# Layer 1's second half in quarters, its first product for two token blocks from seven block products

## The chip, the cores and the metric

The kernel runs on one core of one Trainium2 chip. The metric is the device time of one execution in microseconds (us): 603.91 us, the median of three runs (602.19 to 604.12).

## The reference

```python
attn_out = _attn_ref(**attn_kwargs)          # 2 batches, 8 heads, 768 tokens, head size 64; window of 16 and block maxima
x = attn_out.transpose(0, 2, 1, 3).reshape(B * S, H * D)      # 1536 tokens x 512
...
h = x @ w_in                                 # layer 1: 512 -> 2048
g = h * np.clip(h + 3.0, 0.0, 6.0) / 6.0
x = g @ w_out                                # 2048 -> 512
...
h = x @ w_in                                 # layer 2, other weights
g = h * (1.0 / (1.0 + np.exp(-h)))
return (g @ w_out).astype(np.float32)
```

The weights of both layers arrive as 64-bit floats.

## The kernel before

**Precision.** Every operand of a wide matmul is kept as two 32-bit parts, a high part (a rounded copy) and a low part (value minus high part). A product of two operands is three matmuls, high x high, high x low and low x high, summed in one bank. So `hidden` (line 720), the first product of one slice of 128 hidden units for one block of 512 tokens, is 4 pieces of the inner size 512 times 3 = 12 matmuls of 128x512, issued as two halves of 6. `project` (lines 790 to 817), the second product of that slice, is 4 output groups x 3 = 12 matmuls.

**Stages.** Attention fills the first part; its results are turned into layer 1's input `x` (lines 699 to 717). Then come the two layers. A layer's 2048 hidden units are 16 slices, in two halves of 8. `STEPS` lists (layer, half, first token, tokens, slice) for all 96 pieces of work. Layer 1's first half runs block by block over its 8 slices, and so does its second half, over the token blocks 2, 0, 1. Layer 2 runs its halves in quarters of 4 slices: a quarter goes through blocks 2, 0, 1 before the next quarter starts. One `chunk` is the stretch of pieces that is summed in the same four accumulator banks; when it ends, the banks are emptied into `acc` in the local memory: `finish` with half 0 copies (ScalarE), `finish` with half 1 adds (VectorE, line 869, with a sixth as factor in layer 1) and for layer 1 also writes the high part of layer 2's input, `finish_lo` (line 880) the low part; `fold` (line 854) adds layer 2's early quarters.

**Seven block products.** In layer 2, blocks 0 and 1 don't go through `hidden`. Two slices of hidden units, split by the two halves of the inner size, are a 2x2 arrangement of weight blocks; the two token blocks, split the same way, are a 2x2 arrangement of inputs. Their product is formed from seven products instead of eight (`FACTORS`, `prod` on line 947), each 2 pieces x 3 = 6 matmuls. Their operands are partly sums: four weight sums per pair of slices (`ssum`, line 915, VectorE, 128x256; high parts `s_hi` on line 934, low parts `s_lo` on line 941) and four token sums per layer (`tsum` on line 897, `t_hi`, `t_lo`, 128x1024). Seven joins on VectorE (`join`, line 971: `u2`, `vee`, `u4`, `c22`, `c21`, `c12`, `c11`) and one copy (`keep`) turn seven products into the four results `k`, `v`, `u`, `d` of a pair. From there `act` (ScalarE, sigmoid or relu), `gate` (VectorE), `gate_hi` (mostly ScalarE) and `gate_lo` (VectorE, line 786) make the two parts of the operand of `project`. Layer 1 applies `act` and `gate` to a bank directly (line 769), the block products' results lie in the local memory (line 764).

**Weights.** `fetch` loads 64-bit words (SP), five steps on ScalarE and VectorE turn them into 32-bit values in `bits`, `conv_hi` copies the high part into a weight buffer and `conv_lo` subtracts (GpSimd on line 467, or VectorE).

**What sets the order.** Nothing is reordered: every engine executes its instructions in the order in which `PROGRAM` lists the operations. `ORDER` is that list, written out in the source; a star sends a copy to VectorE that ScalarE would do, or a `conv_lo` or `normal` to VectorE instead of GpSimd. Eight banks are shared by all products, taken and freed in that order (`Ring`), and so are the buffers of gates (`gs`), values (`rs`) and weights (`ws`). `grow` turns memory that has become free into more of these buffers.

```python
STEPS += [(0, 1, j * WIDE, WIDE, f) for j in BLOCKS for f in range(HALF)]
STEPS += [
    (1, half, j * WIDE, WIDE, q * QUARTER + f)
    for half in range(2)
    for q in range(2)
    for j in BLOCKS
    for f in range(QUARTER)
]
FACTORS = {
    1: ("w", 0, 0, "x", 0, 0),
    2: ("w", 0, 2, "x", 0, 2),
    3: ("s", 3, 0, "x", 1, 2),
...
```

Of the kernel before, what the change touches and what calls it, by code (L numbers as in the profile page):

```python
# [168 lines left out]
hidden 8 1, act 8, conv_sign 16, conv_clamp 16, conv_join 16, finish 0 0 0 2, mix 17, gate 8, hidden 9 1,
hidden 11 1, conv_hi 16, inverse 19, normal 19*, turn 19, mixed_hi 17*, gate_hi 8*, gate_lo 8, load_v 16, mix  # L170
16, keys 21, mixed_hi 16, mixed_lo 16, scores 21, masked 21, turned 19, keys 23*, turn 18, fetch 17, conv_low
17, act 9, gate 9, exps 21, guard 21, hidden 10 0, hidden 10 1, inverse 21, normal 21*, gate_hi 9, gate_lo 9,
grow 1, turned 18, conv_sign 17, load_v 19, mix 19, conv_mag 17, conv_clamp 17, conv_join 17, conv_hi 17*,
# [974 lines left out]
```

## Time and profile before

| | us |
|---|---|
| median of three runs | 603.91 |
| the profiled execution | 602.95 |
| its span (first to last instruction) | 601.1 |
| TensorE busy (3164 matmuls) | 590.1 |
| VectorE busy | 476.4 |
| ScalarE busy | 261.3 |
| GpSimd busy | 86.1 |

The profile names engines PE (TensorE), DVE (VectorE), ACT (ScalarE), POOL (GpSimd) and SP (transfers); PEld is TensorE's loading of weights. Busy is the time in which at least one instruction of the engine ran; a matmul's recorded duration overlaps the next one's, so the pace of a stream is read from starts. The granted TensorE clock is 1.00 in every slice of 20 us from 20 us on.

### The profile page before, as it was taken

Reading aid. Unit: us, or ns where it says so; the run is one execution under the profiler, and the core shown is the slowest. Engines: PE = TensorE matmul, PEld = TensorE weight load, DVE = VectorE, ACT = ScalarE, POOL = GpSimd, SP = SyncE. Lnnn points to the kernel's source line nnn. Section 1 sums busy time; section 2 is a strip of 40 time slices with the busy share of each in tenths; the row PEclk is TensorE's granted clock in tenths of the full one; section 3 lists DMA queues with packets and bytes.
Section 4 is the critical chain, followed back from the end, with each engine's and each line's share of the span. In section 5 each row is a group of like instructions: output and inputs, shape, how many; then the busy total and the mean of one; then the engine's idle time right before and its main releaser. Section 6 shows DMA issues by size and latency. Waiting matters only on the chain.

```text
span 601.1 us, 8713 instructions
## 1 busy us (share of the span) xinstructions
PE 590.1 (98%) x3164; PEld 489.4 (81%) x3164; DVE 476.4 (79%) x1047; ACT 261.3 (43%) x614; POOL 86.1 (14%) x97
## 2 busy tenths in 40 slices
PE   7899999999999999999999999999999999999997
PEld 7778788888888888888888888888888788888886
DVE  4999999587697867955446799998989888988865
ACT  4898778664322324421223435344434233421330
POOL 3583330200001012000000100010100310121000
PEclk9999999999999999999999999999999999999999
DMA  9999965231323223202000202123123122120023
GB/s 249 262 216 259 213 168 111 71 99 26 95 70 106 81 95 106 71 5 66 1 0 1 70 1 70 36 70 106 39 67 105 37 70 71 31 75 1 1 87 123
DMA packets 69051, 51.56 MB, mean 86 GB/s; under 512 B 36368, under 2 KB 63504, under 8 KB 69008
## 3 DMA queue, kind: packets, MB, share of 16 engines
q1 hardware_dynamic: 69008, 51.01, 31.5%
q8 instruction: 25, 0.41, 0.3%
q14 instruction: 18, 0.15, 0.1%
HBM read 47.85 MB, written 3.15 MB: 85 GB/s over the span
## 4 chain that ended last, share of the span: by engine, by line
PE 86%; DVE 7%; ACT 4%; DMA 1%; issue 1%; SPq 0%; DVEq 0%; ACTq 0%
PE bank L730 27%; PE bank L806 22%; PE bank L809 19%; PE bank L966 11%; PE bank L622 2%; PE bank L691 2%; PE bank L679 1%; PE bank L517 1%; DMA early_w<-in_k_dram 1%; DVE g L786 1%; PE bank L1063 1%; ACT early_units L651 1%; ACT early_w L651 1%; DVE kmax L531 1%; DVE early_w L637 1%
## 5 line engine op out<-in xcount | busy, mean ns | idle before, releaser
L730 PE MATMUL bank<-x,w 128*128 128x512 f32 x576 | 139.8, 392 | 0.0
L806 PE MATMUL bank<-g,w 128*128 128x512 f32 x576 | 137.9, 392 | 0.0
L809 PE MATMUL bank<-w,g 128*128 128x512 f32 (+1 forms) x588 | 136.3, 385 | 0.4 <-DVE g L786 0.3
L809 PEld LDWEIGHTS bank<-w,g 128*128 128x128 f32 x588 | 108.7, 188 | 23.3 <-DVE g L786 1.3
L806 PEld LDWEIGHTS bank<-g,w 128*128 128x128 f32 x576 | 107.1, 188 | 22.2
L730 PEld LDWEIGHTS bank<-x,w 128*128 128x128 f32 x576 | 107.2, 188 | 22.0 <-DVE x L714 0.2
L467 POOL TENSOR_TENSOR w<-bits,w 128x512 fp32r<-128x512 f32 x26 | 36.1, 1391 | 324.0 <-ACT w L463 161.4
L786 DVE TENSOR_TENSOR g<-r,g 128x512 fp32r<-128x512 f32 x72 | 52.9, 739 | 16.9 <-ACT g L780 15.5
L759 ACT ACTIVATE r<-bank 128x512 f32<-128x512 f32 x60 | 35.4, 596 | 67.2 <-PE bank L730 50.6
L423 ACT ACTIVATE mag<-words 128x512 f32<-128x512 f32 x64 | 42.9, 671 | 43.8 <-DVE bits L445 16.9
L769 DVE SCALAR_TENSOR_TENSOR r<-r,bank 128x512 f32<-128x512 f32 x48 | 32.7, 683 | 21.2 <-ACT r L759 21.0
L780 ACT CAST g<-r 128x512 fp32r<-128x512 f32 x43 | 26.7, 621 | 52.1 <-PE bank L806 16.1
L730 PE MATMUL bank<-x_late,w 128*128 128x512 f32 x192 | 44.7, 389 | 0.0
L730 PEld LDWEIGHTS bank<-x_late,w 128*128 128x128 f32 x192 | 36.0, 188 | 7.5
L966 PE MATMUL bank<-w,x 128*128 128x512 f32 x144 | 35.7, 389 | 0.0
L452 DVE SCALAR_TENSOR_TENSOR bits<-words,bits 128x512 uint32<-128x512 uint32 x48 | 34.8, 725 | 0.7
L439 DVE TENSOR_SCALAR mag<-mag 128x512 f32<-128x512 f32 x64 | 28.5, 445 | 7.9 <-ACT mag L423 7.5
L445 DVE SCALAR_TENSOR_TENSOR bits<-mag,bits 128x512 uint32<-128x512 uint32 x48 | 33.1, 689 | 1.0
L966 PEld LDWEIGHTS bank<-w,x 128*128 128x128 f32 x144 | 27.0, 188 | 5.6
L651 ACT ACTIVATE early_w<-early_w,stat 128x120 f32<-128x120 f32 x72 | 27.5, 385 | 4.0 <-DVE stat L637 3.9
L467 POOL TENSOR_TENSOR w<-cst,w 128x512 fp32r<-128x512 f32 x10 | 14.3, 1425 | 88.2 <-ACT w L463 44.0
L432 DVE TENSOR_SCALAR bits<-words 128x512 uint32<-128x512 uint32 x48 | 22.0, 460 | 3.5 <-DMA words<-in_moe_w_in_dram 1.8
(144 smaller groups left out, 768.3 us busy)
## 6 DMA issues: line engine op xcount, KB each, us to landing
words<-in_moe_w_in_dram SPq DMA_DIRECT2D x32, 512.0 KB, 3.9
words<-in_moe_w_out_dram SPq DMA_DIRECT2D x32, 512.0 KB, 3.4
early_r<-in_v_dram SPq DMA_DIRECT2D x15, 192.0 KB, 4.5
out_dram<-acc SPq DMA_DIRECT2D x11, 256.0 KB, 2.0
early_w<-in_q_dram SPq DMA_DIRECT2D x10, 256.0 KB, 6.0
stage<-in_k_dram SPq DMA_DIRECT2D x3, 512.0 KB, 5.2
stage<-in_v_dram SPq DMA_DIRECT2D x3, 512.0 KB, 7.2
early_w<-in_v_dram SPq DMA_DIRECT2D x3, 512.0 KB, 5.5
```

Source lines behind the costliest of these rows:

```text
L423: nc.scalar.activation(out=out, in_=low_high(h)[:, 1].bitcast(F32), func=AF.Abs, scale=EXP_SHIFT)
L445: nc.vector.scalar_tensor_tensor(out=bits, in0=mags.use(h).bitcast(U32), scalar=3, in1=bits, op0=ALU.logical_shift_left, op1=ALU.bitwise_or,)
L452: nc.vector.scalar_tensor_tensor(out=bits, in0=low_high(h)[:, 1], scalar=0x80000000, in1=bits, op0=ALU.bitwise_and, op1=ALU.bitwise_or,)
L467: eng.tensor_tensor(out=w_half(h, 1), in0=bitss.use(h).bitcast(F32), in1=w_half(h, 0).bitcast(F32), op=ALU.subtract,)
L651: nc.scalar.activation(out=pr[:, hp], in_=pr[:, hp], func=AF.Exp, scale=-1.0, bias=st[:, 0, hp : hp + 1], accum_out=st[:, 1, hp : hp + 1],)
L730: nc.tensor.matmul(ps[:, :n], w[:, a, kk * P : (kk + 1) * P], x[:, o // SUB : (o + n) // SUB, b, kk, :], start=(m == 0), stop=(m == last),)
L759: nc.scalar.activation(out=r, in_=ps, **kind)
L769: nc.vector.scalar_tensor_tensor(out=r, in0=r, scalar=6.0, in1=ps, op0=ALU.min, op1=ALU.mult)
L786: eng.tensor_tensor(out=g[:, 1, cols], in0=r[:, cols], in1=g[:, 0, cols].bitcast(F32), op=ALU.subtract)
L806: nc.tensor.matmul(ps[:, o : o + n], lhs, g[:, b, shift : shift + n], **flags)
L809: nc.tensor.matmul(ps[:, : len(cols)], g[:, a, rows], rhs, **flags)
L966: nc.tensor.matmul(ps, lhs, rhs, start=(i == 0), stop=(i == 5))
```

## The change

Layer 1's second half takes the form that layer 2 has. Its `STEPS` run in quarters, so that it has six chunks instead of three; the three of the first quarter are added to `acc` by a new operation `sixth`. Its 8 slices are 4 pairs, and for blocks 0 and 1 `hidden` gives way to `prod` and the joins. `act` and `gate` then work on stored values, `gate` with the clamp at 6. Layer 1's input exists only as high and low parts, so its token sums are formed from these, 3 instructions for the sums 1 and 3 and 2 for the sums 2 and 4, in halves of 512 columns; layer 2's token sums are cut into the same halves. The weight sums' buffer is the part of block 1's input that no product needs any more, in layer 1 its own and in layer 2 again layer 2's. The value buffers are made earlier (`grow 6`), the separate buffers for token sums are gone, and the rest of `ORDER` is a new list.

```diff
-STEPS += [(0, 1, j * WIDE, WIDE, f) for j in BLOCKS for f in range(HALF)]
 STEPS += [
-    (1, half, j * WIDE, WIDE, q * QUARTER + f)
-    for half in range(2)
+    (layer, half, j * WIDE, WIDE, q * QUARTER + f)
+    for layer, half in ((0, 1), (1, 0), (1, 1))
...
-    return (layer, half, o // WIDE, f // QUARTER) if layer else (layer, half, o // WIDE)
+    return (layer, half, o // WIDE, f // QUARTER if layer + half else 0)
...
-    if s[0] and s[2] == 0 and s[4] % 2 == 0:
+    if s[0] + s[1] and s[2] == 0 and s[4] % 2 == 0:
...
-act 16, gate 16, gate_hi 16*, gate_lo 16, conv_low 24, conv_sign 24, hidden 24 0, hidden 24 1, fetch 26, act 21, gate
...
+            r = rs.use(("temp", i))
+            if STEPS[i][0] == 0:
+                nc.vector.scalar_tensor_tensor(
+                    out=h, in0=r, scalar=6.0, in1=h, op0=ALU.min, op1=ALU.mult
+                )
...
+    def add_sixth(ps, part):
+        nc.vector.scalar_tensor_tensor(
+            out=part, in0=ps, scalar=1.0 / 6.0, in1=part, op0=ALU.mult, op1=ALU.add
+        )
+
+    def sixth(j, m):
+        add_sixth(*gathered((0, 1, j, 0), m)[:2])
...
+    OPERANDS = {1: ((1, 0), (0, 0)), 2: ((1, 1), 1), 3: ((1, 1), (1, 0)), 4: ((0, 1), 2)}
+
+    def tsum(layer, a, n):
+
+        x, y = OPERANDS[a]
+        out = rs.take(("t", layer, a, n), 3 if a < 3 else 2)
+
+        def whole(j, half):
+            return acc_part(0, j * KD + 2 * half + n)
+
+        def split(j, half, ab):
+            return xs[0][j][:, :, ab, 2 * half + n, :].bitcast(F32)
+
+        old = None if a % 2 else rs.use(("t", layer, y, n))
+        if layer:
+            terms = [(out, whole(*x), old if a % 2 == 0 else whole(*y), ALU.subtract)]
+        else:
+            o = halves(out)
+            y = [halves(old)] if a % 2 == 0 else [split(*y, ab) for ab in range(2)]
+            terms = [(o, split(*x, 0), y[0], ALU.subtract), (o, o, split(*x, 1), ALU.add)]
+            terms += [(o, o, t, ALU.subtract) for t in y[1:]]
+        for o, s, t, op in terms:
+            nc.vector.tensor_tensor(out=o, in0=s, in1=t, op=op)
...
+            if p % HALF == HALF // 2 * (1 - layer):
+                assert not sb.held
+                x = second_x(1) if layer else xs[0][1]
+                sb.free[:] = [[x[:, n, b, 0:2, :] for n in range(2) for b in range(2)]]
...
-                rhs = xs[1][m][:, :, b, kr + kk, :]
+                rhs = xs[p // HALF][m][:, :, b, kr + kk, :]
```

Lines move: in the changed kernel `hidden` is line 740, `prod` line 1005, `join` line 1014, `project` lines 822 and 825, the additions of `finish` and `sixth` line 871, `tsum` line 935, `t_lo` line 946, `ssum` line 968, `s_lo` line 982, `gate` 776 to 789, `gate_lo` line 802.

TensorE in layer 1's second half, before: the end of block 0 and the start of block 1 (`x_0` and `x_1` are their inputs, `g` the gated operand of the second product, `w` weights).

```order
L730 MATMUL bank_75<-x_1_65,w_487 128x512 x6
L730 MATMUL bank_78<-x_1_65,w_1056 128x512 x6
L730 MATMUL bank_74<-x_1_65,w_87 128x512 x12
L730 MATMUL bank_76<-x_1_65,w_1579 128x512 x12
L730 MATMUL bank_77<-x_1_65,w_1458 128x512 x12
L730 MATMUL bank_72<-x_1_65,w_86 128x512 x12
```

And now, the third pair's products (6 matmuls each), with projections of blocks 0 and 1 and a half `hidden` of block 2 (`x_late`) between them.

```order
L1005 MATMUL bank_72<-x_0_64,w_485 128x512 x6
L822 MATMUL bank_76<-g_92,w_488 128x512 x3
L822 MATMUL bank_74<-g_92,w_488 128x512 x3
L1005 MATMUL bank_75<-w_87,x_1_65 128x512 x6
L1005 MATMUL bank_73<-w_86,x_1_65 128x512 x6
L1005 MATMUL bank_72<-w_486,w_487 128x512 x6
L740 MATMUL bank_79<-x_late,w_487 128x512 x6
L1005 MATMUL bank_74<-w_1640,x_1_65 128x512 x6
L1005 MATMUL bank_76<-x_1_65 128x512 x6
```

Slices of a block that came one after the other are now products of a pair, spread between projections.

VectorE in the same half, before, where the second half's work for block 2 ends: gates (lines 769, 786), evictions (line 869), weight conversion (439, 452, 432).

```order
L769 SCALAR_TENSOR_TENSOR r_93<-r_93,bank_73 128x512
L786 TENSOR_TENSOR g_91<-r_1832,g_91 128x512
L786 TENSOR_TENSOR g_1831<-r_1832,g_1831 128x512
L467 TENSOR_TENSOR w_486<-bits_67,w_486 128x512
L780 CAST g_92<-r_93 128x512
L786 TENSOR_TENSOR g_92<-r_93,g_92 128x512
L869 SCALAR_TENSOR_TENSOR acc_1838<-bank_79,acc_1838 128x512
L869 SCALAR_TENSOR_TENSOR acc_1838<-bank_78,acc_1838 128x512
L452 SCALAR_TENSOR_TENSOR cst<-words_70,cst 128x512
```

And now, while the first quarter of block 2 (`acc_1879`) is emptied: the stretch from the join `vee` of pair 5 (the sixth row) on, which the prediction counts.

```order
L1014 TENSOR_TENSOR values<-bank_75,values 128x512
L871 SCALAR_TENSOR_TENSOR acc_1879<-bank_78,acc_1879 128x512
L776 SCALAR_TENSOR_TENSOR values<-values 128x512
L871 SCALAR_TENSOR_TENSOR acc_1879<-bank_73,acc_1879 128x512
L776 SCALAR_TENSOR_TENSOR r_93<-values,r_93 128x512
L1014 TENSOR_TENSOR values<-bank_72,r_1751 128x512
L968 TENSOR_TENSOR words_69<-words_69,bits_67 128x256
L968 TENSOR_TENSOR words_69<-bits_67,words_69 128x256
L1014 TENSOR_TENSOR values<-bank_76,values 128x512
L982 TENSOR_TENSOR x_1_65<-words_69,x_1_65 128x256
L871 SCALAR_TENSOR_TENSOR acc_1879<-bank_79,acc_1879 128x512
L802 TENSOR_TENSOR g_91<-values,g_91 128x512
```

Joins, weight sums and the evictions of `sixth` stand between the gates, which now read stored values.

VectorE at the seam of the layers, before: evictions of blocks 0 and 1 (line 869), token sums of 1024 columns (904, 911), low parts of layer 2's input (882).

```order
L869 SCALAR_TENSOR_TENSOR acc_1838<-bank_77,acc_1838 128x512
L911 TENSOR_TENSOR w_1794<-sums,w_1794 128x1024
L882 TENSOR_TENSOR x_1_2761<-acc_1838,x_1_2761 128x2x256
L904 TENSOR_TENSOR sums<-acc_1838,sums 128x1024
L904 TENSOR_TENSOR sums<-acc_1290,sums 128x1024
L911 TENSOR_TENSOR w_1458<-sums,w_1458 128x1024
```

And now, the stretch that begins with the eviction of the last product.

```order
L871 SCALAR_TENSOR_TENSOR acc_1879<-bank_72,acc_1879 128x512
L871 SCALAR_TENSOR_TENSOR acc_1290<-bank_77,acc_1290 128x512
L871 SCALAR_TENSOR_TENSOR acc_1290<-bank_76,acc_1290 128x512
L871 SCALAR_TENSOR_TENSOR acc_1879<-bank_74,acc_1879 128x512
L935 TENSOR_TENSOR r_1751<-acc_1290 128x512
L935 TENSOR_TENSOR values<-acc_1879,r_1751 128x512
L935 TENSOR_TENSOR values<-acc_1879,acc_1290 128x512
L904 TENSOR_TENSOR x_0_2951<-acc_1290,x_0_2951 128x2x256
L935 TENSOR_TENSOR r_1751<-acc_1879,acc_1290 128x512
```

The sums come in halves, with the low parts of block 0's input (`x_0`, line 904) among them.

## Rows read from the trace of the kernel before

**Rows 1.** The page's engine table: busy us, share of the span, instructions.

```profile
PE 590.1 (98%) x3164; PEld 489.4 (81%) x3164; DVE 476.4 (79%) x1047; ACT 261.3 (43%) x614; POOL 86.1 (14%) x97
```

**Rows 2.** Slices of 20 us: busy us of PE, PEld, DVE, ACT, POOL (instructions); clock; DMA.

```profile
0.00:20.00 20.00, 15.73 (x100) 14.89 (x100) 11.68 (x35) 10.18 (x21) 8.13 (x21) 0.91 1.05 253
20.00:40.00 20.00, 18.35 (x234) 15.36 (x233) 18.80 (x85) 19.53 (x83) 13.45 (x16) 1.00 1.06 242
40.00:60.00 20.00, 18.62 (x168) 15.27 (x167) 19.79 (x67) 18.03 (x53) 10.21 (x10) 1.00 1.14 245
...
440.00:460.00 20.00, 20.00 (x90) 16.57 (x89) 19.70 (x40) 6.50 (x13) 1.32 (x1) 1.00 0.23 78
...
580.00:600.00 20.00, 17.99 (x91) 15.16 (x89) 10.69 (x18) 2.96 (x5) 0.00 (x0) 1.00 0.29 106
```

**Rows 3.** TensorE's waits from 200 us on: line, releaser, us in total, times, longest.

```profile
PE bank L809 <- DVE g L786: 0.3, 1, 0.3
```

**Rows 4.** Pieces of the chain that ended last: start, us, engine and line, instructions.

```profile
311.12 13.60 PE bank L730 x60
...
381.84 6.80 PE bank L966 x30
```

**Rows 5.** Longer stretches, same columns as rows 2.

```profile
140.00:340.00 200.00, 200.00 (x956) 164.76 (x955) 134.26 (x251) 62.54 (x118) 13.84 (x10) 1.00 0.19 59
200.00:340.00 140.00, 140.00 (x620) 115.86 (x619) 90.33 (x159) 42.86 (x78) 9.95 (x7) 1.00 0.16 49
340.00:580.00 240.00, 239.58 (x1056) 197.67 (x1055) 212.72 (x383) 89.52 (x160) 23.88 (x17) 1.00 0.17 53
440.00:540.00 100.00, 99.58 (x438) 81.80 (x437) 89.99 (x167) 33.47 (x61) 15.08 (x11) 1.00 0.21 63
```

**Rows 6.** VectorE in order of time, with a full queue: start, us, instruction.

```profile
440.53 0.42 DVE L943 TENSOR_TENSOR x<-words,x 128x256 fp32r<-128x256 f32 x1
440.86 0.42 DVE L932 TENSOR_TENSOR words<-bits 128x256 f32<-128x256 f32 x1
...
449.44 0.68 DVE L975 TENSOR_TENSOR sums<-bank,sums 128x512 f32<-128x512 f32 x1
450.04 0.68 DVE L452 SCALAR_TENSOR_TENSOR bits<-words,bits 128x512 uint32<-128x512 uint32 x1
...
451.24 0.42 DVE L432 TENSOR_SCALAR cst<-words 128x512 uint32<-128x512 uint32 x1
451.57 0.68 DVE L975 TENSOR_TENSOR sums<-bank,sums 128x512 f32<-128x512 f32 x1
```

**Rows 7.** VectorE's groups by shape: busy us, mean ns, idle before and releaser.

```profile
L975 DVE TENSOR_TENSOR sums<-bank,sums 128x512 f32<-128x512 f32 x25 | 17.1, 685 | 2.6 <-PE bank L966 2.2
L869 DVE SCALAR_TENSOR_TENSOR acc<-bank,acc 128x512 f32<-128x512 f32 x12 | 8.1, 688 | 13.4 <-PE bank L806 13.4
L911 DVE TENSOR_TENSOR w<-sums,w 128x1024 fp32r<-128x1024 f32 x4 | 4.9, 1220 | 0.0
```

**Rows 8.** Engines in order of time around the wait of rows 3.

```profile
464.64 1.32 POOL L467 TENSOR_TENSOR w<-bits,w 128x512 fp32r<-128x512 f32 x1 [20.74 <-PE bank L809]
...
464.83 1.68 DVE L764 TENSOR_TENSOR sums<-sums,r 128x512 f32<-128x512 f32 x1
465.92 1.75 POOL L467 TENSOR_TENSOR w<-cst,w 128x512 fp32r<-128x512 f32 x1
466.43 1.79 DVE L786 TENSOR_TENSOR g<-r,g 128x512 fp32r<-128x512 f32 x1
...
468.28 3.94 PE L809 MATMUL bank<-w,g 128*128 128x512 f32 x14 [0.28 <-DVE g L786]
```

**Rows 9.** GpSimd's groups from 200 to 580 us, columns as in rows 7.

```profile
L467 POOL TENSOR_TENSOR w<-bits,w 128x512 fp32r<-128x512 f32 x15 | 21.0, 1403 | 251.9 <-ACT w L463 144.6 <-DVE w L463 86.5 <-PE bank L809 20.7
L467 POOL TENSOR_TENSOR w<-cst,w 128x512 fp32r<-128x512 f32 x9 | 13.0, 1440 | 66.5 <-ACT w L463 44.0 <-DVE r L975 14.1 <-DVE w L463 8.3
```

More of the change, by code (lines that the diff above doesn't have):

```diff
@@ L169 @@
[L169 to L173, printed above, removed]
@@ new lines @@
+24, conv_mag 24, act 25, gate 25, gate_hi 25*, gate_lo 25, conv_low 24, conv_sign 24, project 21 0, prod 4 2,
+c11 4, fetch 25, prod 4 7, vee 4, u4 4, ssum 5 2, prod 4 3, s_hi 5 3*, project 21 1, project 23 0, project 23
+1, ssum 5 4, s_hi 5 1, conv_clamp 24, act 28, conv_lo 23, conv_join 24, s_hi 5 2, c22 4, s_hi 5 4, s_lo 5 2,
+conv_mag 25, conv_low 25, conv_sign 25, act 33, conv_clamp 25, c12 4, conv_lo 20, t_hi 0 4 0*, t_lo 0 4 0,
+hidden 26 0, hidden 26 1, act 26, s_lo 5 1, finish 0 0 2 1, fetch 26, conv_low 26, prod 5 6, s_lo 5 3,
@@ new lines @@
+0 2 2, conv_hi 26, conv_join 27, conv_hi 27*, conv_lo 27, project 26 1, gate_lo 27, conv_low 28, conv_sign 28,
+conv_mag 28, project 25 1, conv_clamp 28, fetch 30, conv_join 28, project 27 0, project 27 1, sixth 2 2,
+conv_hi 28*, conv_lo 28, gate_hi 28, gate_lo 28, keep 5, u2 5, prod 5 2, c11 5, sixth 2 1, act 30, gate 30,
+prod 5 3, prod 5 5, sixth 2 0, act 29, gate 29, gate_hi 30, gate_hi 29, prod 5 7, vee 5, conv_lo 24, hidden 36
+0, ssum 6 2, ssum 6 4, s_hi 6 4, c22 5, s_lo 6 4, prod 5 4, sixth 2 3, project 28 0, gate_lo 30, project 30 0,
@@ new lines @@
+36*, act 38, project 31 0, sixth 0 0, project 31 1, sixth 0 3, project 32 0, gate_hi 33, gate_lo 33,
+conv_clamp 31, project 32 1, gate 34, gate_hi 34*, conv_sign 31, conv_join 31, gate_lo 34, sixth 0 2, act 35,
+gate 35, fetch 32, conv_low 32, project 33 0, gate 38, conv_mag 32, sixth 0 1, hidden 37 0, project 33 1,
+gate_hi 35, project 34 0, gate_lo 35, prod 6 1, keep 6, conv_sign 32, conv_clamp 32, conv_join 32, conv_hi 30,
+conv_hi 32, gate_lo 36, fetch 33, project 35 0, sixth 1 1, sixth 1 0, conv_mag 33, prod 6 6, u2 6, conv_hi 31,
@@ new lines @@
+gate_lo 38, project 36 0, project 37 0, project 38 0, c12 6, s_hi 7 2, c11 6, act 41, gate 41, s_lo 7 2, act
+44, conv_mag 35, gate 44, act 39, ssum 8 1, ssum 8 2, ssum 8 4, ssum 8 3, conv_lo 34, conv_clamp 35, conv_join
+35, gate 39, keep 7, fetch 37, sixth 1 2, project 36 1, project 38 1, conv_low 37, fetch 36, prod 7 6, gate_hi
+39, gate_lo 39, conv_sign 37, gate_hi 44, act 40, gate_lo 44, conv_mag 36, gate 40, project 39 0, finish 0 1 2
+0, prod 7 7, conv_clamp 36, prod 7 3, u2 7, conv_low 36, conv_sign 36, conv_join 36, conv_mag 37, vee 7,
@@ new lines @@
+56, act 53, gate 53, prod 9 3, gate_hi 53*, gate_lo 53, ssum 10 1, s_hi 10 1, vee 9, c22 9, c21 9, ssum 10 2,
+gate 54, gate_hi 54*, conv_mag 43, conv_clamp 43, act 55, project 53 0, ssum 10 4, gate_lo 54, act 59, gate
+59, project 53 1, s_hi 10 2, fetch 44, conv_lo 42, prod 10 1, hidden 61 0, hidden 61 1, ssum 10 3, s_hi 10 3,
+u4 9, c12 9, act 58, keep 10, gate 55, s_lo 10 3, prod 10 7, s_lo 10 2, prod 10 6, conv_low 43, gate 58,
+conv_sign 43, conv_join 43, act 57, gate_hi 55, conv_low 44, act 61, conv_mag 44, gate_lo 55, fetch 46,
@@ new lines @@
+2*, s_lo 15 2, prod 14 2, c11 14, hidden 87 1, s_hi 15 3*, project 84 0, project 84 1, prod 15 6, act 87, gate
+87, fold 2 0 3, gate_hi 87, gate_lo 87, conv_lo 61, project 86 0, ssum 15 4, s_hi 15 4, project 86 1, conv_low
+63, conv_sign 63, conv_clamp 63, conv_join 63, s_lo 15 4, prod 15 1, gate_lo 85, project 85 0, s_lo 15 3,
+conv_hi 63*, project 85 1, act 88, gate 88, gate_hi 88*, keep 15, u2 15, prod 15 2, c11 15, gate_lo 88,
+conv_lo 63, act 90, project 87 0, project 87 1, finish 1 1 2 1, finish 1 1 2 0, finish 1 1 2 3, gate 90,
@@ L323 @@
+gate_hi 95*, gate_lo 95, close 0, close 1, close 2, finish 1 1 0 3, finish 1 1 1 0, close 3, close 4, finish 1
+1 1 1, finish 1 1 1 2, finish 1 1 1 3, finish 1 1 1 4
 """
@@ L861, in finish @@
     def finish(layer, half, j, m):
-        ps, part, rows, cols = gathered((layer, half, j, half) if layer else (layer, half, j), m)
+        ps, part, rows, cols = gathered((layer, half, j, half), m)
         if half == 0:
@@ L868, in finish @@
         elif layer == 0:
-            nc.vector.scalar_tensor_tensor(
-                out=part, in0=ps, scalar=1.0 / 6.0, in1=part, op0=ALU.mult, op1=ALU.add
-            )
+            add_sixth(ps, part)
             if only_in_sums(j, m):
```

327 lines of the change are left out of this document (151 added, 176 removed).

## The prediction

> **What bounds the kernel now.** I read the page's engine table first. TensorE is busy for 590.1 of 601.1 us, VectorE for 476.4, ScalarE for 261.3 [rows 1]. A busy TensorE is not by itself a bound, so I looked next at where it stands idle: in the table of 20 us slices it misses 4.3, 1.6 and 1.4 us in the first three slices (attention starting up) and 2.0 us in the last, where only evictions and transfers are left [rows 2]. Of what is left, the list of TensorE's waits from 200 us on holds one entry, 0.3 us behind a VectorE instruction of line 786 [rows 3]. So from 60 us to 598 us TensorE streams without a break, and the chain of work that ended last is made of TensorE pieces nearly throughout. The time then follows from the number of wide matmuls and the time from one start to the next. Two pieces of the chain give that time: 60 matmuls in 13.60 us and 30 in 6.80 us, both 0.2267 us each, one for line 730 and one for the block products of line 966 [rows 4]. (Their mean duration of some 390 ns is longer because they overlap.)
>
> The second thing to see is VectorE. Over 140 to 340 us it is busy 134.3 of 200 us, over 340 to 580 us, where layer 2's block products run, 212.7 of 240 us [rows 5]. In one slice, 440 to 460 us, it reached 19.70 of 20.00 us and TensorE still missed nothing [rows 2].
>
> **What the change removes.** In layer 1's second half the first product of token blocks 0 and 1 took 2 blocks x 8 hidden slices x 12 matmuls = 192 on line 730. They become 4 pairs x 7 products x 6 matmuls = 168. The order of instructions agrees: 768 to 576 there and 336 to 504 in the block products, and no other group of TensorE changes its count. So 24 matmuls of 128x512 go, and 24 x 0.2267 = **5.44 us** of TensorE [rows 4].
>
> On that price the Trainium skill speaks against the change: the page "TensorE: Matmul & The Clock Gate", section "Back-to-back issue gap", gives about 131 ns per 512-column matmul for a sustained stream of weight load and matmul. An estimate by that page would be 24 x 0.131 = 3.1 us. The rows above measure the same thing and differ, so they decide.
>
> **What it adds to VectorE.** The durations of rows overlap by a little, so I price an instruction by the distance from its start to the next start where the queue is full: 0.60 us for 128x512, 0.33 us for a 128x512 tensor-scalar or a 128x256 tensor-tensor [rows 6].
> - 28 more joins of a product with the running sum, 1 more keep on VectorE and 12 new `sixth` (each of the 12 accumulator banks is now emptied a quarter earlier): 41 x 0.60 = 24.6 us. They are the instructions of lines 975 and 869, 685 and 688 ns [rows 7].
> - Token sums of layer 1, which must be formed from high and low parts: 3 + 2 + 3 + 2 = 10 instructions for each of two halves, 20 x 0.60 = 12.0 us. Their low parts and those of layer 2, cut in two: 16 x 0.60 instead of 4 x 1.14 (the 1.22 us row of line 911 less the same overlap) = 5.0 us [rows 6, 7]; layer 2's sums themselves come out equal (8 x 0.60 against 4 x 1.14). High parts on VectorE: 6 x 0.33 instead of one of 0.6, 1.4 us.
> - Weight sums: 16 x 0.33 and their low parts 16 x 0.33 = 10.6 us; 5 more high parts on VectorE at 0.2 us (estimate from the 128x256 casts, less the overlap), 1.0 us.
> - Twelve instructions fewer elsewhere (weight casts and subtractions, attention), about -4.7 us by the same prices.
> The sum is 24.6 + 12.0 + 5.0 + 1.4 + 10.6 + 1.0 - 4.7, with 0.2 for the equal pair, = **50 us**. VectorE would stand at 526 of some 596 us, 88%. The 16 gates of the block products only move from a bank to a stored value, 0.60 us either way. ScalarE gains 3 keeps, 7 high parts of token sums, 11 of weight sums and 6 copies taken over from VectorE, by its rows about 12 us on 261: it stays below half and hides it. GpSimd gets one weight subtraction more (37 for 36), SP issues the same 129 transfers; neither ends a wait of TensorE in the trace from 200 us on [rows 3].
>
> **Is there room for those 50 us?** If all of it fell between 200 and 340 us, VectorE would need 90.3 + 50 = 140 us there, and TensorE has only 140 - 5.4 = 134.6: that would not fit [rows 5]. Spread from 140 us on it is 184 of 194.6 us. The new order says which. I counted VectorE's row from the first join (pair 4) to the last `finish` of layer 1: 143 instructions at 0.60, 76 at 0.335 and 4 at 0.2 are 112.1 us. TensorE's row between the same two places holds 546 matmuls, 123.8 us. So 90.5% full, like layer 2 today (88.6%), and 11.7 us to spare; some token sums were moved ahead, in among the last units of attention.
>
> Averages do not show a late single piece, so I also took the two stretches where VectorE has most to do between a result of TensorE and the next need for it. First, from the join `vee 5` to the low part of hidden slice 35: 54 VectorE instructions, 32 at 0.60, 20 at 0.335 and 2 at 0.2, 26.3 us; TensorE has 120 matmuls, 27.2 us, in between. Spare: 0.9 us. Second, the seam of the layers: from the eviction of layer 1's last product to the last low half of layer 2's input for block 0, 21 instructions, 12.1 us, against 63 matmuls, 14.3 us. Spare: 2.2 us. Both hold, narrowly.
>
> What can eat the 0.9 us is in the trace. At 464.64 us GpSimd starts a weight subtraction, a second at 465.92; the VectorE additions beside them take 1.68 and 1.79 us instead of 0.69, and at 468.28 TensorE starts after the only idle time it has in this half, 0.28 us [rows 8]. So a GpSimd subtraction costs VectorE between 0 and 1.1 us, and a piece with about 2 us less than planned made TensorE wait 0.3 us. From 200 to 580 us there are 15 + 9 of them [rows 9], some eight in 124 us: 0 to 8.8 us on 112.1, still inside 123.8.
>
> The Trainium skill names the mechanism: the page "SBUF — State Buffer", section "Who interferes with whom", says that a VectorE instruction with two SBUF inputs contends with a GpSimd instruction that reads SBUF and that the later one blocks fully. By that rule the added token sums, weight sums, their low parts and the moved gates (84 instructions) are exposed and the joins, which read a bank, are not; the trace agrees as far as the two stretched additions had both inputs in SBUF. This bears on the rivals below.
>
> For added waiting I take 0.6 us, twice what the trace shows; ends: 0.3 us less than now (the wait at 468 us goes with the new order) and 3.6 us, three or four such places at 1.1 us. The profiled run took 602.95 us, 601.1 of span and 1.85 around it: 602.95 - 5.44 + 0.6 = 598.1. The median shown, 603.91, stands 0.96 above that run, so the forecast is **599.1 us**.
>
> **The rivals.**
> - VectorE lets part of it go: the wait at some narrow places sums to 1.5 to 3.6 us. For: the spare 0.9 us and the 84 exposed instructions. Against: layer 2 runs the same scheme at 88.6% with 0.3 us. 600.0 to 602.1 us.
> - Nothing to measure: waits of 3.6 to 7.2 us, because the stretched instructions fall together in pairs 5 to 7. 602.1 to 605.7 us. What a measurement of this kernel tells from no change is about 0.3%, 1.8 us.
> - Slower, VectorE becomes the bound of layer 1's second half: every GpSimd subtraction there costs the full 1.1 us (120.9 us) and VectorE idles the 10.0% it idles in 440 to 540 us [rows 5], so it needs 134.3 us where TensorE has 123.8: 10.5 us late, 603.91 - 5.44 + 10.5 = 609.0 us. It decides from 7.2 us late on, 18.9 us of stretch and idling on top of the 112.1. Against it: that idle time is mostly VectorE having nothing ready, and in 440 to 460 us it idled 0.3 us.
> - The change doing less than it says, fewer than 24 matmuls gone: excluded by the count in the order.
>
> **How the numbers follow.** Forecast (waits up to 1.5 us) 0.66, partly given back 0.17, nothing to measure 0.11, slower 0.06. The first two are faster by over 0.3%: 0.83. The low end is the fastest run shown less the matmuls and the wait that may go, 602.19 - 5.44 - 0.28 = 596.5; the high end takes in the second case, 602.1. About 0.17 lies above it and little below.
>
> **What would show it.** TensorE's busy time falls to about 585 us and its starts stay 0.2267 us apart; VectorE rises to 520 to 530 us; TensorE's waits from 200 us on stay below 1.5 us and name VectorE's `gate_lo` or token sums; the start up to 60 us and the tail from the last projections are unchanged. I am wrong if VectorE's slices between 220 and 345 us stand at 19.5 or more while TensorE's stand below 20, or if waits appear at the seam of the layers.

## The result and the profile after

The changed kernel takes 597.47 us (median of 4 runs, 595.56 to 598.21) where the kernel before took 603.4 us (4 runs, 602.19 to 604.12): a ratio of 0.9899, with a 95% interval of 0.9869 to 0.9929. The forecast was 599.1 us, in a range of 596.5 to 602.1. The profiled run of the changed kernel took 597.93 us, 596.2 us of it the span.

The page's engine table of the changed kernel, columns as in [rows 1]:

```profile
PE 585.7 (98%) x3140; PEld 487.0 (82%) x3140; DVE 521.6 (87%) x1154; ACT 270.4 (45%) x641; POOL 92.8 (16%) x103
```

TensorE has 24 matmuls fewer and is busy 4.4 us less, VectorE is busy 45.2 us more, where some 50 were forecast. What TensorE waits for from 60 us on (line and what ended the wait; us in total, times, longest):

```profile
PE bank L527 <- DMA early_w<-in_k_dram: 0.5, 1, 0.5
```

That one lies in attention's start, before 70 us; behind it TensorE does not wait once, and the 0.3 us that [rows 3] hold are gone. A piece of the chain that ended last, in the block products of layer 2 (start, us, instructions), keeps the pace of [rows 4], 6.80 / 30 = 0.2267 us:

```profile
375.15 6.80 PE bank L1005 x30
```

The slices in which layer 1's second half runs (columns as in [rows 2]) and a longer stretch:

```profile
240.00:260.00 20.00, 20.00 (x90) 16.57 (x89) 17.08 (x32) 6.22 (x11) 6.24 (x4) 1.00 0.17 53
260.00:280.00 20.00, 20.00 (x90) 16.55 (x89) 19.22 (x39) 7.87 (x14) 0.00 (x0) 1.00 0.21 60
280.00:300.00 20.00, 20.00 (x90) 16.55 (x89) 19.30 (x36) 7.80 (x15) 1.30 (x1) 1.00 0.23 75
300.00:320.00 20.00, 20.00 (x90) 16.57 (x89) 19.27 (x36) 10.93 (x21) 2.60 (x2) 1.00 0.34 104
320.00:340.00 20.00, 20.00 (x90) 16.57 (x89) 19.79 (x38) 8.22 (x15) 1.30 (x1) 1.00 0.08 27
...
200.00:335.00 135.00, 135.00 (x597) 111.80 (x596) 126.38 (x236) 54.52 (x101) 14.30 (x10) 1.00 0.22 67
```

VectorE (third engine of a row) is busy 126.4 of 135 us from 200 to 335 us, 94%, where it had 64% in [rows 5], and over 96% from 260 us on. TensorE still misses nothing. So the 24 matmuls came out of the time in full, and the added VectorE work is hidden. By how little it is hidden is what most of the experiments are about.

One thing did change that was not meant to: the start. The attention group of 32 small matmuls that I use as a landmark between start-up and the rest begins at 107.44 us before and at 108.70 us now. The second row, and the clock in the third (0.83), show where (TensorE's pieces in order of time, with the idle time before each, then a slice with the columns of [rows 2]):

```profile
18.29 1.15 PE L632 MATMUL bank<-early_units,early_w 128*128 128x120 f32 x8 [1.04 <-POOL early_units L625]
21.15 3.77 PE L632 MATMUL bank<-early_w,early_w 128*128 128x120 f32 x16 [1.72 <-DVE early_w L625]
...
20.00:40.00 20.00, 18.85 (x196) 16.61 (x196) 16.46 (x78) 16.87 (x69) 12.30 (x15) 0.83 1.01 222
```

These 16 matmuls take 3.77 us, and the granted clock of the slice is 0.83, where [rows 2] have 1.00. In the trace of before the same 16 take 2.04 us:

```profile
21.70 2.04 PE L622 MATMUL bank<-early_w,early_w 128*128 128x120 f32 x16 [1.50 <-DVE early_w L615]
```

Of the time behind the landmark, the span now has 596.2 - 108.70 = 487.5 us, against 601.1 - 107.44 = 493.7 before: 6.2 us less, 5.44 from the matmuls, 0.28 from the wait, 0.4 from elsewhere. This distance, free of start-up, is used below beside the medians; it comes from one profile of each kernel.

### The profile page after: what moved, and what is told of

The parts are those of the page before. It is cut to its first block, busy times and chain, and to the rows that moved or that the text cites. A ratio compares the mean times of both kernels' runs of the same rounds, so it can differ in the third digit from the quotient of the medians.

```text
span 596.2 us, 8823 instructions
## 1 busy us (share of the span) xinstructions
PE 585.7 (98%) x3140; PEld 487.0 (82%) x3140; DVE 521.6 (87%) x1154; ACT 270.4 (45%) x641; POOL 92.8 (16%) x103
## 4 chain that ended last, share of the span: by engine, by line
PE 93%; DVE 3%; ACT 2%; DMA 1%; issue 0%; SPq 0%; DVEq 0%
PE bank L825 22%; PE bank L822 22%; PE bank L740 21%; PE bank L1005 19%; PE bank L632 3%; PE bank L701 2%; PE bank L689 1%; DMA early_w<-in_k_dram 1%; PE bank L527 1%; PE bank L1102 1%; DVE kmax L541 1%; ACT early_w L661 1%; DVE early_units L647 0%; PE bank L595 0%; PE bank L576 0%; DVE x L724 0%
## 5 line engine op out<-in xcount | busy, mean ns | idle before, releaser
L740 PE MATMUL bank<-x,w 128*128 128x512 f32 x384 | 95.2, 394 | 0.0
L740 PEld LDWEIGHTS bank<-x,w 128*128 128x128 f32 x384 | 70.9, 188 | 14.5
L1005 PE MATMUL bank<-w,x 128*128 128x512 f32 x216 | 53.5, 389 | 0.0
L1005 PEld LDWEIGHTS bank<-w,x 128*128 128x128 f32 x216 | 40.5, 188 | 8.4
L802 DVE TENSOR_TENSOR g<-values,g 128x512 fp32r<-128x512 f32 x53 | 36.3, 687 | 2.7 <-ACT g L796 1.7
L796 ACT CAST g<-values 128x512 fp32r<-128x512 f32 x30 | 18.6, 620 | 40.4 <-PE bank L822 14.4
L1005 PE MATMUL bank<-x,w 128*128 128x512 f32 x144 | 36.5, 389 | 0.0
L802 DVE TENSOR_TENSOR g<-r,g 128x512 fp32r<-128x512 f32 x43 | 29.5, 687 | 5.9 <-ACT g L796 5.2
L462 DVE SCALAR_TENSOR_TENSOR bits<-words,bits 128x512 uint32<-128x512 uint32 x48 | 33.3, 693 | 0.8
L1005 PEld LDWEIGHTS bank<-x,w 128*128 128x128 f32 x144 | 27.0, 188 | 5.6
L796 ACT CAST g<-r 128x512 fp32r<-128x512 f32 x28 | 17.4, 621 | 30.7 <-PE bank L825 12.0
```

Of the source, the lines that this page charges most:

```text
L462: nc.vector.scalar_tensor_tensor(out=bits, in0=low_high(h)[:, 1], scalar=0x80000000, in1=bits, op0=ALU.bitwise_and, op1=ALU.bitwise_or,)
L740: nc.tensor.matmul(ps[:, :n], w[:, a, kk * P : (kk + 1) * P], x[:, o // SUB : (o + n) // SUB, b, kk, :], start=(m == 0), stop=(m == last),)
L796: copier("gate_hi", i)(out=g[:, 0, cols], in_=value(i)[:, cols])
L802: eng.tensor_tensor(out=g[:, 1, cols], in0=r[:, cols], in1=g[:, 0, cols].bitcast(F32), op=ALU.subtract)
L1005: nc.tensor.matmul(ps, lhs, rhs, start=(i == 0), stop=(i == 5))
```

## The experiments

All are ratios to the kernel before as it ran in the same series (603.4 us beside the changed kernel, 602.8 to 603.0 us beside the others), each with its 95% interval.

| run | median us | ratio | landmark to end, us |
|---|---|---|---|
| before | 602.8 | 1 | 493.7 |
| after | 597.47 | 0.9899 [0.9869, 0.9929] | 487.5 |
| e1_before_drop24 | 596.57 | 0.9891 [0.9878, 0.9904] | 488.2 |
| e2_after_add24 | 602.93 | 0.9999 [0.9987, 1.001] | 492.8 |
| e3_after_drop24 | 593.43 | 0.9845 [0.9827, 0.9863] | 485.0 |
| e4_dve12 | 605.48 | 1.0045 [1.0028, 1.0062] | 496.2 |
| e9_before_dve12 | 605.6 | 1.005 [1.0033, 1.0067] | 497.1 |
| e10_unstar | 597.97 | 0.9921 [0.9903, 0.9938] | 489.5 |
| e7_drop24_unstar | 597.69 | 0.9907 [0.9884, 0.993] | 488.8 |
| e8_dve12_unstar | 606.3 | 1.0053 [1.0037, 1.0069] | 497.5 |
| e11_dve4 | 601.07 | 0.9977 [0.9959, 0.9994] | 492.5 |
| e13_drop24_noclamp | 591.93 | 0.9808 [0.9786, 0.9831] | 482.7 |
| e14_dve12_noclamp | 604.9 | 1.0034 [1.0019, 1.005] | 495.3 |
| e12_warm | 595.38 | 0.987 [0.9848, 0.9891] | 487.5 |

**Is it the 24 matmuls?** First the kernel before with 24 matmuls left out and nothing added, then the changed kernel with 24 added back.

```
         # e1, before: in the first products of layer 1's second half
+            if STEPS[i][:2] == (0, 1) and STEPS[i][2] < 2 * WIDE and (m == 10 or m == 7 and i % 2):
+                continue
         # e2, after: in the block products of layer 1's second half
+            if p < HALF and k < 7 and i == 1:
+                nc.tensor.matmul(ps, lhs, rhs, start=False, stop=False)
```

> The kernel before with 24 of the 192 matmuls of layer 1's second half for blocks 0 and 1 left out (one low-part term in each of 16 pieces, two in 8 of them); order, VectorE's work and everything else as before. It is the removed TensorE work alone. Theory (TensorE streams without a break, each matmul is worth its start-to-start distance of 0.2267 us): 5.4 us faster than before, ratio 0.991. Rival (a matmul is worth less than its distance, since the instructions around it wait on other engines): 3 us or less, ratio 0.995 or more.

> The changed kernel with 24 matmuls put back: in 24 of the 28 block products of layer 1 one low-part term is added twice, so TensorE has as many wide matmuls as before. What is left of the difference to before is the new order, the 50 us of VectorE work and nothing else. Theory (VectorE's additions are hidden): within 1 us of before, rather 0.3 to 0.8 us faster because the wait of 0.28 us at 468 us is gone; ratio 0.9985 to 1.000. Rival (the new order saves or costs time of its own): more than 1.5 us either way, ratio below 0.9975 or above 1.0025.

Measured: 596.57 and 602.93 us, both close to their theories. From the landmark on, the first is 5.5 us shorter than before (24 x 0.2267 = 5.44), the second 5.3 us longer than after. With the same number of matmuls the old and the new scheme cost the same within 0.2%: the added 45 us of VectorE, the new order and the smaller pieces are worth nothing that shows either way, and the gain is the matmuls at 0.2267 us each. The 131 ns that the Trainium skill gives in "TensorE: Matmul & The Clock Gate", section "Back-to-back issue gap", would have made it, by estimate, 3.1 us; these runs, like the rows, do not agree with that here.

**How much room had VectorE left?** Two runs push on the margin from either side: 24 more matmuls out of the block products, and 12 idle instructions more on VectorE, an in-place maximum of the accumulator with itself behind each of the 12 new evictions.

```
         # e3, in the block products
+            if p < HALF and k < 7 and i == 4:
+                continue
         # e4, in `sixth`
-        add_sixth(*gathered((0, 1, j, 0), m)[:2])
+        ps, part = gathered((0, 1, j, 0), m)[:2]
+        add_sixth(ps, part)
+        nc.vector.tensor_tensor(out=part, in0=part, in1=part, op=ALU.max)
```

> The changed kernel with 24 more matmuls left out, one low-part term in 24 of the 28 block products of layer 1. It asks how much TensorE work could still go before VectorE, 95% busy from 220 to 345 us, is late. Theory (TensorE alone bounds, VectorE has 6 us to spare there): all of 5.4 us more, about 11.3 us faster than before, ratio 0.981. Rival (VectorE is next: 118.8 us of work in 119.6 us): TensorE waits 1.5 to 4 us there, 7 to 10 us faster than before, ratio 0.9835 to 0.988, with waits on VectorE in the trace between 220 and 345 us.

> The changed kernel with one more VectorE instruction (128x512, both inputs in the local memory, in place, maximum of a value with itself) behind each of the 12 new evictions of line 871: 12 x 0.60 = 7.2 us more between 255 and 340 us. Theory of the prediction (0.9 us spare at the narrow places, 6.2 us of VectorE idle in 125 us): the spare time is used up, TensorE waits 1 to 3 us, ratio to before 0.992 to 0.996. Rival (VectorE has much more room than its busy share says): no wait, same ratio as the changed kernel, 0.990.

Measured: 593.43 us, 2.5 us off the span behind the landmark instead of 5.4 (4.0 us by the medians), which is the rival's range; and 605.48 us, 8.7 us on it for 7 to 8 us of VectorE work, above both ranges. TensorE's waits from 60 us on, first of the run with fewer matmuls, then of the one with more VectorE work:

```profile
PE bank L822 <- DVE g L802: 1.4, 5, 0.4
...
PEld bank L822 <- DVE g L802: 3.4, 5, 0.8
```

```profile
PE bank L822 <- DVE g L802: 5.3, 4, 2.9
PE bank L822 <- ACT g L796: 1.4, 1, 1.4
```

Both wait mostly for the low half of a gate (line 802) on VectorE, the first at five places between 238 and 326 us. An average room of 11.7 us, as the prediction had it, would have swallowed either. It is not there.

**The amount of work, or its place?** The same 12 maxima went into the kernel before, behind its 12 evictions of the same half, where VectorE has time; and the changed kernel got only the first 4.

```
         # e9, before, in `finish` of layer 1's second half, behind the eviction
+            nc.vector.tensor_tensor(out=part, in0=part, in1=part, op=ALU.max)
         # e11, after, in `sixth`
+        if j == 2:
+            nc.vector.tensor_tensor(out=part, in0=part, in1=part, op=ALU.max)
```

> The kernel before with one in-place maximum of a 128x512 tile with itself (which changes nothing) on VectorE behind each of the 12 evictions of the first layer's second half: 12 x 0.6 to 0.7 us = 7.2 us and more of VectorE work at the very place where the same 12 cost the changed kernel 8.7 us. Theory (it is VectorE's fullness in the changed kernel that made them dear): before, VectorE is busy 64% of the stretch 200 to 340 us, so nothing shows, 602.8 us, ratio 0.998 to 1.002. Rival (they cost time because they stand in the chain from a block's eviction to its half's use, whatever VectorE has to do): 606 to 611 us.

> The changed kernel with only the 4 maxima behind the evictions of the first output block of the second half (around 250 to 262 us), 2.4 to 2.8 us of VectorE work. Theory (the stretch has no room for the chain of evictions to be longer, about 1 us): 598.5 to 600.5 us, with waits for a gate half near 262 us. Rival (some 11 us of room, as the average of the stretch says, and the 12 only passed its end): 597.2 to 598 us, no wait from 60 us on.

Measured: 605.6 us, 2.7 us more than before where I expected nothing; and 601.07 us, 3.6 us for 4 instructions of 0.7 us. All the ranges were missed, and neither result fits an account by VectorE's average busy share. The rows of VectorE and TensorE around 260 us explain the second. In the changed kernel (start, us, instruction, idle time before):

```profile
250.75 0.69 DVE L871 SCALAR_TENSOR_TENSOR acc<-bank,acc 128x512 f32<-128x512 f32 x1 [1.19 <-PE bank L822]
...
259.29 0.68 DVE L871 SCALAR_TENSOR_TENSOR acc<-bank,acc 128x512 f32<-128x512 f32 x1
259.89 0.68 DVE L802 TENSOR_TENSOR g<-values,g 128x512 fp32r<-128x512 f32 x1
...
259.39 5.60 PE L822 MATMUL bank<-g,w 128*128 128x512 f32 x24
```

and with the 4 maxima (line 879):

```profile
251.74 0.69 DVE L871 SCALAR_TENSOR_TENSOR acc<-bank,acc 128x512 f32<-128x512 f32 x1 [1.19 <-PE bank L822]
...
256.13 0.92 DVE L879 TENSOR_TENSOR acc<-acc 128x512 f32<-128x512 f32 x1
256.98 1.78 DVE L776 SCALAR_TENSOR_TENSOR values<-values 128x512 f32<-128x512 f32 x1
...
260.38 1.75 PE L822 MATMUL bank<-g,w 128*128 128x512 f32 x7
265.02 5.77 PE L822 MATMUL bank<-g,w 128*128 128x512 f32 x17 [2.89 <-DVE g L802]
```

At 250.75 us VectorE has just waited 1.2 us for TensorE's bank; from there on it works through a full queue to `gate_lo 30`, done at 260.57 us. TensorE needs it behind 7 matmuls, at 259.39 + 7 x 0.2267 = 260.98 us. The spare time there is 0.4 us. The 4 maxima (and a VectorE instruction stretched to 1.78 us beside a GpSimd subtraction) put the gate half 3.4 us later against the same bank, and TensorE waits 2.89 us. The profile is of the slowest of the 12 runs of e11, and its 5.0 us behind the landmark hold 1.6 us of a lower clock behind this wait (last section). In the run with 12 maxima the same place costs 2.88 us. In the kernel before, the maxima cost a wait of 0.8 us at 275.5 us, and waits of 0.6 and 0.4 us at the seam of the layers (the 0.3 us are those of [rows 3]):

```profile
PE bank L806 <- DVE g L786: 0.8, 1, 0.8
PE bank L809 <- ACT g L780: 0.6, 1, 0.6
PE bank L967 <- DVE r L773: 0.4, 1, 0.4
PE bank L809 <- DVE g L786: 0.3, 1, 0.3
```

VectorE stands idle for 4.9 us of the slice around the first, but does not wait from 268.3 to 276.1 us; at the seam a chain of evictions and token sums fills it. The first three rows are from the run with the maxima, the last one is the kernel before without them (columns as in [rows 2]):

```profile
260.00:280.00 20.00, 19.18 (x84) 15.52 (x84) 15.08 (x26) 5.25 (x9) 1.29 (x1) 1.00 0.16 53
...
350.00:360.00 10.00, 10.00 (x45) 8.28 (x45) 9.86 (x13) 3.21 (x5) 0.00 (x0) 1.00 0.01 2
360.00:370.00 10.00, 8.99 (x37) 6.47 (x36) 9.63 (x14) 4.21 (x7) 0.00 (x0) 1.00 0.15 52
...
350.00:360.00 10.00, 10.00 (x46) 8.29 (x45) 9.89 (x12) 4.64 (x7) 0.00 (x0) 1.00 0.01 2
```

So the 12 cost the kernel before, 64% busy on average, about a third of what they cost the changed one, at places where VectorE's queue is full for a while. They stand behind other evictions there (`finish` and not `sixth`), so the runs do not show how much of the 8.7 us is their place and how much the smaller room.

**Take VectorE's work away.** The first try moved 13 casts of the stretch to ScalarE and 4 subtractions of the weight conversion to GpSimd, by striking the stars in the order (as here), in the changed kernel and in the two pushed ones.

```
-6 1, ssum 6 3, project 25 0, conv_hi 25*, fetch 28, conv_lo 25*, conv_low 27, conv_sign 27, fetch 29, finish 0
+6 1, ssum 6 3, project 25 0, conv_hi 25, fetch 28, conv_lo 25, conv_low 27, conv_sign 27, fetch 29, finish 0
```

> The changed kernel with 12 casts of the stretch 205 to 340 us (5 of gate halves, 5 of conversions, the rest of sums) moved from VectorE to ScalarE, and 4 subtractions of the conversion from VectorE to GpSimd: some 13 x 0.42 + 4 x 0.69 = 8 us less on VectorE there. Theory (TensorE binds, with no wait left, so a less full VectorE gives nothing by itself): 597.5 us, ratio 0.989 to 0.992. Rival (the longer way over ScalarE, 0.62 us for 0.42, and GpSimd, 1.46 for 0.69, makes a gate half or a converted weight late): 598.5 to 601 us.

> The run that left out 24 further matmuls of the block products of the first layer's second half (its span fell by 2.4 us and not by 5.4, with some 3 us of waits for VectorE's gate halves and what follows), now with the same 17 instructions moved off VectorE. It leaves those 24 terms out of the result. Theory (in the run with 24 matmuls less VectorE was the bound of the stretch): the lost 3 us come back, 590.5 to 592.5 us, ratio 0.979 to 0.983, waits from 60 us on under 1 us. Rival (what was late there was a chain through ScalarE or the weights, not the amount of VectorE's work): 593 to 596 us.

> The changed kernel with the 12 added maxima behind the second half's evictions (605.5 us without more), now with the 17 instructions moved off VectorE, some 8 us against the 7.2 added. Theory (room on VectorE is what was lacking): back to 597.5 to 599.5 us, ratio 0.990 to 0.995. Rival (the maxima cost by where they stand, or by keeping an accumulator from its reader): 603 to 606 us.

Measured: 597.97, 597.69 and 606.3 us: no gain in the changed kernel, where TensorE now waits 1.4 us for a gate half near 262 us; 4.3 us worse than its counterpart in the second, and 0.8 us worse in the third, both above their two ranges. In these two the granted clock also fell behind the longest wait (2.3 and 3.9 us), and the 17 matmuls after it took 5.76 and 6.50 us; in e4 the same 17 took 4.19 us. The try did not test what it was made for, since it put a new wait on VectorE. VectorE's waits from 195 to 275 us in the first of the three:

```profile
DVE bits L442 <- POOL w L477: 6.0, 2, 4.6
```

That was 1.2 us in the changed kernel: here VectorE cannot begin the next conversion before GpSimd has subtracted from the buffer of the last, and GpSimd itself waits for ScalarE's cast. So these stars are worth more here than their 0.4 to 0.7 us.

The second try leaves out work that no other engine waits for: 17 in-place clamps of the conversion, 0.34 us each.

```
     def conv_clamp(h):
+        if 23 <= h < 40:
+            return
         mag = mags.see(h)
```

> The run that left out 24 further matmuls of the block products, now without the clamp of the converted exponent (in place, 0.34 us of VectorE's time each) in the conversions 23 to 39, those of the stretch 205 to 340 us: 17 x 0.34 = 5.7 us less on VectorE and no longer way for anything else. It leaves out those 24 terms and those 17 clamps. Theory (VectorE was the bound there): the 3 us of waits go, 590.3 to 592 us, ratio 0.979 to 0.982. Rival (a chain in which the clamps play no part): 593 to 594 us.

> The changed kernel with the 12 added maxima behind the second half's evictions (605.5 us), without the 17 clamps of the conversions 23 to 39, which it leaves out: + 12 x 0.6 to 0.7, - 17 x 0.34, so VectorE has 1.5 to 2.5 us more to do than in the changed kernel. Theory (5 to 6 of the 8.7 us that the maxima cost were VectorE's fullness, the 3 us that they also cost in the kernel before are their place in the chain from eviction to use): 599.5 to 602 us. Rival (all of it is their place): 604.5 to 606 us.

Measured: 591.93 us, in the theory's range, and 604.9 us, in the rival's. With 24 matmuls fewer, leaving out the clamps gives back 2.3 us behind the landmark (1.5 us by the medians); TensorE's wait for line 802's gate half (804 in this kernel) falls from 1.4 us in 5 places to

```profile
PE bank L824 <- DVE g L804: 0.4, 1, 0.4
```

so there the amount of VectorE's work was the bound; the wait that is left is at 258 us, the place examined above. With the 12 maxima it is the lesser part. TensorE's waits for gate halves fall from 6.7 us (e4, above) to 5.0:

```profile
PE bank L824 <- DVE g L804: 4.6, 3, 2.9
PE bank L824 <- ACT g L798: 0.4, 1, 0.4
```

The granted clock, which stayed at 1.00 in e4's trace, fell behind the longest of them here (17 matmuls in 5.75 us instead of 4.19) and takes 1.6 us back, so the medians, 0.6 us apart, understate what the clamps are worth. The wait near 260 us is unchanged (start, us, instruction, idle before), because the work saved ahead of it only made VectorE wait longer for TensorE's bank, 1.45 us instead of 1.19:

```profile
250.39 0.69 DVE L873 SCALAR_TENSOR_TENSOR acc<-bank,acc 128x512 f32<-128x512 f32 x1 [1.45 <-PE bank L824]
...
263.67 5.75 PE L824 MATMUL bank<-g,w 128*128 128x512 f32 x17 [2.89 <-DVE g L804]
```

**The start-up.** The last run adds four warming steps, each two small matmuls whose result nobody reads (four instructions in the trace), where TensorE stands idle in the first 21 us.

```
-0, k_copy 0 2 0*, tr q 0 0 1, q_copy 0 0 1 1, ...
+0, k_copy 0 2 0*, tr q 0 0 1, warm 13, q_copy 0 0 1 1, ...
-... keys 2, scores 2, masked 2, ... conv_join 0, scores 3, masked 3, ...
+... keys 2, scores 2, warm 10, masked 2, ... conv_join 0, scores 3, warm 11, warm 12, masked 3, ...
```

> The changed kernel with four more warming steps (two small matmuls each, whose result nobody reads) on TensorE in its start-up: one ahead of the transposes at 12.2 us, one ahead of the scores that start at 18.3 us and two ahead of those that start at 21.2 us, all in stretches in which TensorE idles. Theory (the granted clock falls to its lower level, 1.2 GHz, behind the idle stretches at 11 to 12 us or 17 to 21 us, in one run here and in another there, and costs 1 to 2 us): granted clock 1.00 or nearly in the first 30 us, the landmark at 106 to 107 us instead of 108.6, 595.5 to 596.8 us. Rival (the clock falls whatever stands there, or start-up is bound by VectorE and ScalarE and takes the time back): 597 to 598.5 us.

Measured: 595.38 us (595.05 to 596.02). The rows that answer to those of the changed kernel:

```profile
17.59 1.15 PE L632 MATMUL bank<-early_units,early_w 128*128 128x120 f32 x8 [0.59 <-POOL early_units L625]
18.57 1.06 PE L1092 MATMUL bank<-cst 128*128 128x128 f32 x8
20.46 2.04 PE L632 MATMUL bank<-early_w,early_w 128*128 128x120 f32 x16 [0.82 <-DVE early_w L625]
...
20.00:40.00 20.00, 18.92 (x239) 16.17 (x240) 18.66 (x82) 18.94 (x79) 14.43 (x17) 1.00 1.05 247
```

The clock stays at its upper level, 2.4 GHz (1.00), the 16 matmuls take 2.04 us, the landmark stands at 106.81 us instead of 108.70, and behind it the span is the same 487.5 us. The median lies 0.1 us below the range of the theory. This is the fastest kernel here that leaves nothing out, 1.1% to 1.5% under the kernel before. The mean granted clock is 1.000 in all five of its runs and 0.994 to 0.996 in the four of the changed kernel. Its interval still overlaps that of the changed kernel, and e8, which has the changed kernel's start and no such steps, has its landmark at 106.71 us in its profile; so that the four steps hold the clock in start-up is shown, and that they shorten the time is likely but not shown.

## Why the prediction was right, point by point

- **24 x 0.2267 = 5.44 us of TensorE.** Right within 0.2 us, from both sides (5.5 us in e1, 5.3 us in e2).
- **Some 50 us more on VectorE, hidden.** 45.2 us by the page, 521.6 us against the 526 forecast; hidden in full, as e1 shows: with as many matmuls as the changed kernel and none of this work it takes 596.57 us against 597.47 (488.2 and 487.5 us behind the landmark).
- **Waiting added, 0.6 us.** The term that was mis-sized: nothing was added, and the 0.28 us of [rows 8] went, its lower end. With the median of before at 603.4 in the common series instead of 603.91, that 0.9 and this 0.5 us are 1.4 of the 1.6 us by which the result lies under the forecast. For the profiled run the sum gave 598.1 us and 597.93 came, and that nearness is partly luck: 0.9 us less waiting and 0.4 us from elsewhere stand against a start-up that was 1.3 us longer.
- **GpSimd subtractions, some 8 us of stretching on VectorE's 112.1 at most.** From 220 to 345 us there were 12, and they stretched VectorE by some 2 us in all. Two of the stretched instructions, 0.43 and 0.69 us long where nothing disturbs them:

```profile
220.18 0.78 DVE L796 CAST g<-values 128x512 fp32r<-128x512 f32 x1
...
255.85 1.18 DVE L776 SCALAR_TENSOR_TENSOR r<-values,r 128x512 f32<-128x512 f32 x1
```

  The rule that I cited from the Trainium skill, "SBUF — State Buffer", section "Who interferes with whom", agrees with the second row, which has both inputs in SBUF, and with the joins, none of which is stretched in this stretch. The first row, a cast, has one input and is stretched all the same, beside a subtraction that began at 219.38 us: the 84 instructions that I counted as exposed were not all of them.
- **11.7 us to spare, "Both hold, narrowly".** The average was the wrong step, and it was also mis-sized: from the first join of pair 4 to the end of layer 1's last `finish` (218.86 to 344.40 us) VectorE is busy 119.4 of 125.5 us, 95%, where I counted 112.1 of 123.8. Some 2 us of the difference are the stretching above; some 5 us, by the starts of the rows, are my prices, which hold where the next instruction works on something else. Where it takes up what was just written, the starts lie further apart, 0.47 us here instead of 0.33:

```profile
247.34 0.43 DVE L442 TENSOR_SCALAR bits<-words 128x512 uint32<-128x512 uint32 x1 [1.19 <-POOL w L477]
247.81 0.69 DVE L462 SCALAR_TENSOR_TENSOR bits<-words,bits 128x512 uint32<-128x512 uint32 x1
```

  The pieces were the right step, but I took the wrong piece. The narrowest place found is not `vee 5` to `gate_lo 35` (0.9 us by count) but the one just ahead of it, from the eviction of the first block to `gate_lo 30`, with 0.4 us. The rival in which VectorE becomes the bound was to decide "from 7.2 us late on"; e11 lost 3.6 us to 2.4 to 2.8 us of instructions, and e4 8.7 us to 7 to 8. Its mechanism is real, and it was near: by these rows 1 us more in that one place would have taken back part of the gain.
- **What would show it wrong.** VectorE did pass 19.5 us in one slice, 320 to 340 us, but TensorE missed nothing there, and there was no wait at the seam of the layers.
- **"The start up to 60 us [is] unchanged".** Wrong in the profile by 1.3 us. The granted clock fell at 12 us in the one trace, at 20 us in the other, at 44 us in e2, and the landmark moves with it, by up to 3 us among the profiles that share the changed kernel's start (106.71 to 109.69 us). Where the clock fell at the same places, at 12 and at 22 us, the start of before puts the landmark at 107.53 us (e9) and that of the changed kernel at 107.37 to 108.35 us (five runs). So most of the 1.3 us goes with the clock; whether the change, which moved a few of attention's instructions to GpSimd, has a part in it is not shown.

## What to carry to other kernels

When work is added to a second engine, go through the pieces between a result of the first engine and its next need for the second one, all of them, and take the smallest spare time; an average of 94% busy hides a place with 0.4 us left. Work saved ahead of a wait buys nothing behind it, and moving work off a full engine can put a wait on that engine if the new place is slower. Idle stretches of TensorE that look harmless can cost time behind them through the clock (16 matmuls in 3.77 us instead of 2.04); a few matmuls with no reader, put where it idles anyway, held it here.

## What the hardware did that I had not expected

The granted clock fell to 1.2 GHz behind idle stretches in start-up, in one run here and in another there: 12 to 16 us in the trace of before, 20 to 27 us in that of after. One row of before, then two of after (columns as in [rows 2]); in both traces TensorE had been idle for 1.47 us ahead of its 12 matmuls near 12 us:

```profile
10.00:15.00 5.00, 3.53 (x21) 3.31 (x19) 3.21 (x7) 2.87 (x5) 0.62 (x2) 0.72 1.19 301
...
10.00:15.00 5.00, 3.42 (x28) 3.03 (x28) 4.07 (x8) 3.16 (x6) 0.95 (x3) 1.00 1.18 298
20.00:25.00 5.00, 3.85 (x18) 3.85 (x19) 4.55 (x19) 4.54 (x21) 1.67 (x3) 0.51 1.17 293
```

It also fell in the middle of the kernel behind a wait, and not always. In e11 the 17 matmuls behind the wait of 2.89 us took 5.77 us; in e4, behind one of 2.88 us at the same place, they took

```profile
263.00 4.19 PE L822 MATMUL bank<-g,w 128*128 128x512 f32 x17 [2.88 <-DVE g L802]
```

The granted clock from 264 to 272 us was 0.78 in e11 (first two rows) and 1.00 in e4 (third row, to 268 us):

```profile
264.00:268.00 4.00, 2.98 (x10) 2.38 (x11) 3.93 (x8) 1.50 (x3) 0.00 (x0) 0.79 0.05 8
268.00:272.00 4.00, 4.00 (x16) 3.19 (x15) 3.93 (x9) 1.22 (x2) 0.00 (x0) 0.78 0.42 137
...
264.00:268.00 4.00, 4.00 (x19) 3.26 (x19) 3.93 (x8) 2.37 (x5) 0.00 (x0) 1.00 0.41 131
```

So a wait of 3 us cost 1.6 us more in the one than in the other. Of the other profiles, the clock fell behind the waits of 2.3 us (e7), 2.89 us (e14) and 3.9 us (e8), and not behind 1.4 us (e10). It parts the runs of e11 too: the seven with a mean granted clock of 0.994 took 599.73 to 601.31 us, the five with 0.988 to 0.991 took 602.34 to 604.01 us. What tells e4 from e11 was not found.
